# Key-gradient sums' tiles take the merged turns, and query-major scores are issued ahead of some bursts

## The chip, the cores and the metric

The kernel runs on one core of one Trainium2 chip. The metric is the device time of one execution in microseconds (us). Times before: 2569.83 us, the median of 3 runs (2568.68 to 2576.49). One further execution was taken with the hardware profiler; every row shown below comes from it.

## The reference

The reference computes a block and all of its gradients. The block mixes an attention layer and a long convolution of a state-space layer with a gate, for 2048 tokens of 576 channels:

```
g = sigmoid(sum(x * gate_w))                      # one gate per token
a = attention(x, wqkv, wo)                        # 32 heads of 18 channels, softmax over 2048 keys, no mask
b = long_convolution(u, A, B, C, log_dt) + u * Dskip
out = g * a + (1 - g) * b
```

It returns `out` and the gradients with respect to x, wqkv, wo, the six matrices of the state-space layer, log_dt, Dskip and gate_w, given the gradient of `out`. The change touches only the attention's backward pass. There, for each head, the kernel needs, with S the scores, P = exp(S) and dO the output's gradient (already divided by the softmax sums, with the row's correction in an extra channel):

```
dV = P^T dO        dS = P * (V dO^T)        dQ = dS K * scale        dK = dS^T Q
```

## The kernel before, in words

**Tiling.** The heads go in 8 groups of 4 (`NG`), the queries in 4 blocks of 512 (`NQ`, `KB`). A pair (group, query block) is a unit; there are 32 units (`units`), and each takes 32 steps (`NST`). One loop over `G` (from L1359 on) runs all of them, 1024 steps (`NTOT`) and a drain. The forward half of a unit runs at step `G`, its backward half `OFF` = 39 steps later, so that in the middle of the stage each step holds the forward work of one unit and the backward work of an earlier one. A channel group of one head takes 32 rows of the array, so four heads lie side by side (`row`, `tile_position`).

**One step.** The program writes out the order of each engine by hand (`manual_schedule` for TensorE, ScalarE, VectorE, GpSimd and SP), so the order of the code is the order of each engine's queue. A step issues to TensorE:

1. Key-major scores of the forward half, two heads (kind "P1"; `ps_P<-QaT_g,KaT_g` in the profile's names). ScalarE turns them into `PT` = exp(scores), L1475.
2. The first of two products V dO^T (`p2(0)`, "P2"; `ps_P<-dOaT,VaT_g`).
3. A burst or another insertion that depends on the slot, `slot = (G2 + 1) % 8` with `G2 = G - OFF` (below).
4. Query-major scores of the backward half, recomputed from Q and K, two heads (kind "P3"; `ps_P<-KaT_g,QaT_g`). ScalarE turns them into `eb`, L1480, which the sums of dV read.
5. The second product V dO^T (`p2(1)`), then matmuls left over from a burst (`late`).
6. In four of eight steps (G mod 8 in 0, 3, 4, 7, which are slots 2, 5, 6 and 1) the forward output P V, 4 matmuls (`accO`).

VectorE multiplies each product V dO^T with `PT` and writes `ds` (L1485), two a step; between the two it evacuates what the burst left. SP transposes `ds` by DMA (`dsT<-ds`, L1495), three or four blocks of a tile; the blocks left over go through TensorE and VectorE (`turn`, L1112 and L1118).

**Slots.** Eight steps handle one block of 512 keys of a unit. Slots 0 and 1 hold the two halves of the sums for dV (`dv_half`, `accV`), slots 2 and 3 those for dQ (`dq_half`, `accQ`), slots 5 and 6 those for dK (`dk_half`, `accK`); slots 4 and 7 hold `turn`. In step G mod 32 = 5 the `turn` also transposes the output's gradient (`do_tile`), in step G mod 32 = 2 the forward output is turned instead (`accF`).

**PSUM.** It is fully divided: two score tiles of two banks (`S`, taken in turn by P1 and P3, so that P1 needs the tile that `PT` of the step before has read, and P3 the one that `eb` of the step before has read), two banks for V dO^T (`dP`), one for the forward output (`accO`) and one (`accB`) for all bursts and turns. The first half of a burst can write `accB` only when VectorE has evacuated what was there.

**Gradients of K and V.** The sums over the four query blocks of a group are held in SBUF, in `dvacc` and `dkacc` (float32, 4 buffers each, one for each block of 512 keys). With the last query block, the evacuation adds the final part and writes bfloat16 into the two halves of the `dvacc` tile. `store_grad` (L1080) then lets SP turn both with one DMA transpose (L1083, the "merged turn"), and GpSimd packs each half into `dtk` (L1088) and stores it (L1089), 4 and 6 steps after the turn was issued (`packs`). The turn is issued 11, 19, 18 and 18 steps after the sum's last burst for the four key blocks of a group (2 steps in the last group). It is written to `gT`, of which there is one buffer. The dQ of the last two units go the same way.

Of the kernel before, what the change touches and what calls it, by code (L numbers as in the profile page):

```python
# [11 lines left out]
BF = mybir.dt.bfloat16  # L12
F32 = mybir.dt.float32
# [4 lines left out]
P = 128  # L18


def build(tc, aps, dbg_aps=None, stages=("s1", "attn", "post", "s4", "final")):
# [39 lines left out]
    with ExitStack() as gctx:  # L61
# [889 lines left out]
        if "attn" in stages:  # L951
# [7 lines left out]
            with ExitStack() as ctx:  # L959
# [117 lines left out]

                    return t_.bitcast(BF)[:, 0:KB]

                def store_grad(gb, g, whichs, t0):  # L1080
                    n = len(whichs)
                    gT = work.tile([P, 2 * TPQ, 4, HP], BF, tag="gT", bufs=1, name="gT")[:, 0:n * TPQ]
                    nc.sync.dma_start_transpose(out=gT.rearrange("p t a b -> p t (a b)"), in_=gb)  # L1083

                    def pack(x):
                        c0 = whichs[x] * D + g * 4 * DH
                        dtk = work.tile([P, TPQ, 4, DH], BF, tag="dtk", bufs=2, name="dtk")
                        nc.gpsimd.tensor_copy(dtk, gT[:, x * TPQ:(x + 1) * TPQ, :, 0:DH])  # L1088
                        nc.gpsimd.dma_start(dqkv_d[:, t0:t0 + TPQ, c0:c0 + 4 * DH], dtk.rearrange("p t a b -> p t (a b)"))  # L1089
                    for x in range(n):  # L1090
                        packs.append((now[0] + 4 + 2 * x, lambda x=x: pack(x)))
                    packs.sort(key=lambda e: e[0])
# [51 lines left out]
                def gb_tile():  # L1144

                    U, g, b = gq.pop(0)
                    gb = U.pop("dqa")
                    dtk = work.tile([P, TPQ, 4, DH], BF, tag="dtk", bufs=2, name="dtk")
# [17 lines left out]
                def at(n, f):  # L1166
                    todo.setdefault(n, []).append(f)

                def accB(name):
                    return apsp.tile([P, KB], F32, tag="accB", name=name)  # L1170

                fill_r = ident_bf.unsqueeze(1).to_broadcast([P, 4, P])
# [56 lines left out]
                def dk_half(g, b, kq, h, acc):  # L1229
                    U = UN[(g, b)]  # L1230
                    o_ = acc[:, 2 * h * P:2 * (h + 1) * P]
                    for qb in range(TPQ):
                        for j in range(4):
                            mm(o_[HP * j:HP * (j + 1), :].rearrange("p (a b) -> p a b", b=P), lhsT=grp_t[g]["Qtok", b][:, qb, HP * j:HP * (j + 1)],
                               rhs=U["dsT", 2 * kq + h][:, :, j * TPQ + qb, :], start=(qb == 0), stop=(qb == TPQ - 1), tile_position=(0, HP * j))

                    def ev():
                        if b == 0:
                            DKV[("k", g, kq)] = work.tile([P, KB], F32, tag="dkacc", bufs=4, name="dkacc")
                            nc.vector.tensor_copy(DKV[("k", g, kq)], acc)  # L1240
                            return
                        a_ = o_ = DKV[("k", g, kq)]
                        if b == NQ - 1:
                            DKV.pop(("k", g, kq))
                            o_ = DKV[("v", g, kq)].bitcast(BF)[:, KB:2 * KB]
                        nc.vector.tensor_tensor(o_, a_, acc, op=A.add)
                    return ev
# [111 lines left out]
                for G in range(NTOT + OFF + 24):  # L1359
# [34 lines left out]
                    evs, late = [], []  # L1394
                    slot = (G2 + 1) % 8
                    m_ = (G2 - (7, 8, 8, 8, 8, 8, 8, 0)[slot]) // 8
                    if ("f1", G) in todo:
                        acc = apsp.tile([P, KB], F32, tag="accO", name="accF")
                        evs.append(todo.pop(("f1", G))[0](acc))
                        e_done[0] += 1.4  # L1400
                    elif G == NST + 5:
                        evs.append(turn(*do_tile(UN[units[0]])))
                    elif 0 <= m_ < NTOT // 8:
                        u_, kq = divmod(m_, NQ)
                        g, b = units[u_]
                        if slot in SLOTS:
                            nm, burst, h = SLOTS[slot]
                            if h == 0:
                                acc = accB("acc" + nm)
                                fill(acc, NFILL[nm])  # L1410
                                burst(g, b, kq, 0, acc)
                            else:
                                evs.append(burst(g, b, kq, 1, acc))
                                if nm == "Q" and kq == NQ - 1 and u_ < NU - 2:
                                    gq.append((UN[(g, b)], g, b))
                                elif nm == "Q" and kq == NQ - 1:
                                    at(("pre", G + 2), lambda g=g, b=b: store_grad(UN[(g, b)].pop("dqa"), g, (0,), b * TPQ))
                                elif nm == "K" and b == NQ - 1:
                                    at(("pre", G + (2 if g == NG - 1 else (11, 19, 18, 18)[kq])), lambda g=g, kq=kq: store_grad(DKV.pop(("v", g, kq)).bitcast(BF), g, (2, 1), kq * TPQ))
                        else:  # L1420
                            p = 2 * kq + (slot == 4)
                            t_, o_ = ds_tiles((g, b), p) if by_pe((g, b), p) else ([], [])
                            if p == 1 and gq:
                                t2, o2 = gb_tile()
                                t_, o_ = t2 + t_, o2 + o_
                            if G % NST == 5 and G // NST - 1 < NU:
                                t2, o2 = do_tile(UN[units[G // NST - 1]])
                                t_, o_ = t2 + t_, o2 + o_
                            evs.append(turn(t_, o_))
                    if r2:  # L1430
                        g, b, s2 = r2
                        T = grp_t[g]
                        U = UN[(g, b)]
                        par_ = (s2 + OFF) % 2
                        kq, ii = s2 // 8, (s2 % 8) // 2
                        ps = s_pair("P3")
                        if not r1 and s2 % 2:
                            fill(ps[:, 1, :], 1)
                        for x, w in enumerate((KT, KB)):
                            row(ps[:, x, KB - KT if x == 0 else 0:KB], T["QaT", b][:, ii * P:(ii + 1) * P], T["KaT", kq][:, 0:w], par_ + 2 * x)  # L1440
                        rows.append(("P3", g, b, (kq, ii), par_, ps))
                        p2(1)
                    for f in late:
                        f()
# [519 lines left out]
```

## Time and profile before

| What | Value |
|---|---|
| Median of 3 runs | 2569.83 us |
| Profiled execution, its own time | 2574.3 us |
| Its span | 2572.5 us |
| TensorE busy (weight loads apart) | 2246.0 us, 87% |
| VectorE busy | 2277.3 us, 89% |
| ScalarE busy | 2257.6 us, 88% |
| GpSimd busy | 1825.5 us, 71% |
| Granted TensorE clock, mean | 0.976 |

In the profile PE is TensorE, DVE VectorE, ACT ScalarE, POOL GpSimd, SPq the queue of SP that issues DMAs. Row groups give: line, engine, operation, output and inputs by the program's names, shapes, count; then busy us, mean ns of one; then the idle time of the engine just before them and what ended it. A timeline row gives start and duration in us, the engine, the line, the operation, and in brackets the idle time before it and its releaser. All matmuls of the helper `mm` have line 30; they are told apart by their tiles. A duration on ScalarE runs from the start to the last write, and consecutive ones overlap. The first `PT` starts at 124.76 us, the first `eb` at 178.39 us, the last `eb` ends at 1983.6 us; before that stage lie projections, behind it the state-space gradients and the output.

### The profile page before, as it was taken

The page shows a single profiled execution, that of the slowest core. Times are in us where ns is not written, and L with a number is a line of the kernel's source. Part 1 is how long each engine was busy: PE and PEld are TensorE (multiplying, and loading weights), DVE is VectorE, ACT ScalarE, POOL GpSimd, SP SyncE. Part 2 cuts the span into 40 slices and gives each one's busy share as a digit, 9 for nine tenths or more (in the row PEclk, how much of TensorE's full clock was granted, in tenths as well). Part 3 has the DMA queues.
Part 4 walks back from the last instruction along what each step waited for, and adds up shares of the span by engine and source line. Part 5 has one row for each costly group of instructions (what it writes and reads, how often), then busy time and mean ns, then how long its engine had stood idle before and what let it go on. Part 6 is the DMA issues. An engine that isn't in the chain of part 4 may idle for free. (4 is left out here: it accounts for less than half of the span.)

```text
span 2572.5 us, 72343 instructions
## 1 busy us (share of the span) xinstructions
PE 2246.0 (87%) x28463; PEld 1164.1 (45%) x28463; DVE 2277.3 (89%) x4121; ACT 2257.6 (88%) x2760; POOL 1825.5 (71%) x2829
## 2 busy tenths in 40 slices
PE   8988888888888888888888888888888899999989
PEld 4433333333333333333333333333334799998666
DVE  4849999899899989999999999999997799999964
ACT  5579999999999999999999999999987699998221
POOL 0379988888899888989888988898851155555331
PEclk8989999999999999999999999999999799999999
DMA  7749999999999999999999999999979799997995
GB/s 236 190 128 182 184 186 203 200 181 196 202 193 188 196 204 187 191 214 191 185 200 196 182 196 209 185 184 200 195 161 207 189 257 259 257 256 239 277 255 130
DMA packets 1272236, 519.05 MB, mean 202 GB/s; under 512 B 1187041, under 2 KB 1224530, under 8 KB 1269590
## 3 DMA queue, kind: packets, MB, share of 16 engines
q1 hardware_dynamic: 1223974, 368.17, 75.1%
q0 software_dynamic: 45904, 140.73, 20.0%
q10 hardware_dynamic: 2016, 5.51, 0.7%
q8 instruction: 223, 3.65, 0.6%
q14 instruction: 119, 0.97, 0.1%
HBM read 149.42 MB, written 96.94 MB: 96 GB/s over the span
## 5 line engine op out<-in xcount | busy, mean ns | idle before, releaser
L1485 DVE TENSOR_TENSOR ds<-ps_P,PT 128x512 bf16<-128x512 f32 x2048 | 1321.1, 684 | 63.1 <-PE ps_P L30 53.0
L1475 ACT ACTIVATE PT<-ps_P 128x1024 bf16<-128x1024 f32 x1024 | 1110.2, 1085 | 16.8 <-PE ps_P L30 14.9
L1480 ACT ACTIVATE eb<-ps_P 128x896 bf16<-128x896 f32 x1024 | 994.5, 972 | 29.5 <-PE ps_P L30 28.9
L30 PE MATMUL ps_P<-dOaT,VaT_g 32*128 32x512 bf16 x2048 | 786.8, 386 | 3.1 <-DVE ds L1485 2.1
L30 PE MATMUL ps_P<-QaT_g,KaT_g 32*128 32x512 bf16 x2048 | 404.5, 385 | 202.5 <-ACT PT L1475 172.5
L507 POOL TENSOR_TENSOR et<-eG,eT 128x448 f32<-128x448 f32 x576 | 543.3, 964 | 10.7
L30 PE MATMUL ps_P<-KaT_g,QaT_g 32*128 32x384 bf16 (+1 forms) x2048 | 402.5, 361 | 4.4 <-ACT eb L1480 0.8
L30 PEld LDWEIGHTS <-KaT_g 32*128 32x128 bf16 x2048 | 161.4, 91 | 491.6 <-issue 468.4
L507 POOL TENSOR_TENSOR Eo<-et,et 128x448 bf16<-128x448 f32 x288 | 327.4, 1137 | 20.5
L30 PE MATMUL accO<-PT,Vtok_g 128*32 128x512 bf16 x2048 | 213.2, 394 | 3.4 <-DMA Vtok_g<-QKV_d 2.9
L30 PEld LDWEIGHTS <-QaT_g 32*128 32x128 bf16 x2048 | 106.9, 91 | 240.3 <-issue 203.4
L30 PE MATMUL accV<-eb,dOa 128*32 128x384 bf16 (+1 forms) x2048 | 184.0, 366 | 9.3 <-DVE dsT L1118 8.5
L30 PEld LDWEIGHTS <-VaT_g 32*128 32x128 bf16 x2048 | 184.2, 91 | 3.6 <-issue 2.0
L30 PE MATMUL accQ<-ds,Ktok_g 128*32 128x512 bf16 x2048 | 158.4, 386 | 24.5 <-DVE dvacc L1208 18.7
L30 PE MATMUL accK<-dsT,Qtok_g 128*32 128x256 bf16 x4096 | 160.8, 278 | 18.9 <-DMA dsT<-ds 16.6
L30 PEld LDWEIGHTS <-dOa 128*32 128x32 bf16 x3072 | 78.1, 95 | 124.0 <-issue 89.3
L1118 DVE COPY dsT<-turn_p 128x1024 bf16<-128x1024 bf16 (+1 forms) x216 | 130.9, 606 | 1.2 <-PE turn_p L1112 1.2
L1112 PE MATMUL turn_p<-ident_bf,ds 128*128 128x128 bf16 x1552 | 126.6, 222 | 1.7 <-DVE gb L1226 1.0
L673 ACT COPY E1e<-etp 128x1024 bf16<-128x1024 bf16 x132 | 125.2, 1065 | 1.9 <-PE etp L672 1.8
L30 PEld LDWEIGHTS <-Qtok_g 128*32 128x32 bf16 x4096 | 87.6, 96 | 86.5 <-issue 72.9
L507 POOL TENSOR_TENSOR et<-eT 128x32 f32<-128x32 f32 (+3 forms) x288 | 116.1, 423 | 11.4
L560 POOL DMA_DIRECT2D E_d<-Eo x144 | 85.1, 591 | 42.8 <-POOL Eo L507 42.8
(306 smaller groups left out, 3796.8 us busy)
## 6 DMA issues: line engine op xcount, KB each, us to landing
E_d<-Eo POOLq DMA_DIRECT2D x144, 256.0 KB, 3.7
E1n<-E_d POOLq DMA_DIRECT2D x30, 1024.0 KB, 6.5
T0w<-Kp_d SPq DMA_DIRECT2D x18, 1024.0 KB
xs<-xb_d POOLq DMA_DIRECT2D x28, 512.0 KB, 10.3
dsT<-ds SPq DMA_TRANSPOSE x512
dqkv_d<-dtk POOLq DMA_DIRECT2D x96, 72.0 KB, 4.4
Md_d<-mst SPq DMA_DIRECT2D x18, 288.0 KB
skw<-Md_d SPq DMA_DIRECT2D x72, 64.0 KB
```

The lines of the kernel that those rows point to most:

```text
L30: return nc.tensor.matmul(out, lhsT=lhsT, rhs=rhs, start=start, stop=stop, **kw)
L507: nc.gpsimd.tensor_tensor(out, a, b, op=op)
L560: nc.gpsimd.dma_start(E_d[:, q // EQ, 0:EQ * 2 * P], Eo.pop(q).rearrange("p c r n -> p (c r n)"))
L673: copy(E_[:, 4 * q:4 * q + 4], pt_)
L1112: nc.tensor.transpose(pt_[:, x, qb, :], t_[:, qb * P:(qb + 1) * P], ident_bf)
L1118: (nc.scalar.copy if NTOT <= now[0] < NTOT + OFF else nc.vector.tensor_copy)(o_(), src_)
L1475: nc.scalar.activation(U["PT"][i, j // 2], ps, ACT.Exp)
L1480: nc.scalar.activation(e, ps.rearrange("p x q -> p (x q)")[:, KB - KT:2 * KB], ACT.Exp)
L1485: nc.vector.tensor_tensor(U["ds"][i][:, j, :], ps, U["PT"][i, j // 2][:, j % 2, :], op=A.mult)
```

## The change

It has two parts.

**Turns.** `store_grad` takes an optional tile `into`. The four merged turns of a group are written into the `dkacc` tile of the same key block, viewed as bfloat16 (its float32 content has been read by the last addition); `dk_half` keeps that tile under the key `("t", g, kq)` for it. `gT` is left for the two dQ turns and is half as large. `dtk` has 3 buffers in place of 2. The turns are issued 11, 13, 17 and 17 steps after the last burst in place of 11, 19, 18 and 18.

**Scores.** Part 3 of a step becomes a function `bursts`. Where the step has a backward half and its slot is 0, 2 or 5 (first half of a burst), or G mod 32 is 5, the query-major scores are issued first, then the burst, then the second product V dO^T. In all other steps the order is as it was. The order on ScalarE and VectorE is unchanged.

```diff
-                def store_grad(gb, g, whichs, t0):
+                def store_grad(gb, g, whichs, t0, into=None):
                     n = len(whichs)
-                    gT = work.tile([P, 2 * TPQ, 4, HP], BF, tag="gT", bufs=1, name="gT")[:, 0:n * TPQ]
+                    if into is None:
+                        gT = work.tile([P, TPQ, 4, HP], BF, tag="gT", bufs=1, name="gT")
+                    else:
+                        gT = into.bitcast(BF).rearrange("p (t a b) -> p t a b", a=4, b=HP)
                     nc.sync.dma_start_transpose(out=gT.rearrange("p t a b -> p t (a b)"), in_=gb)
...
-                        dtk = work.tile([P, TPQ, 4, DH], BF, tag="dtk", bufs=2, name="dtk")
+                        dtk = work.tile([P, TPQ, 4, DH], BF, tag="dtk", bufs=3, name="dtk")
...
                         if b == NQ - 1:
-                            DKV.pop(("k", g, kq))
+                            DKV[("t", g, kq)] = DKV.pop(("k", g, kq))
                             o_ = DKV[("v", g, kq)].bitcast(BF)[:, KB:2 * KB]
...
-                    if ("f1", G) in todo:
-                        acc = apsp.tile([P, KB], F32, tag="accO", name="accF")
...
+                    def bursts():
+                        nonlocal acc
+                        if ("f1", G) in todo:
+                            acc = apsp.tile([P, KB], F32, tag="accO", name="accF")
...
-                                    at(("pre", G + (2 if g == NG - 1 else (11, 19, 18, 18)[kq])), lambda g=g, kq=kq: store_grad(DKV.pop(("v", g, kq)).bitcast(BF), g, (2, 1), kq * TPQ))
+                                        at(("pre", G + (2 if g == NG - 1 else (11, 13, 17, 17)[kq])), lambda g=g, kq=kq: store_grad(DKV.pop(("v", g, kq)).bitcast(BF), g, (2, 1), kq * TPQ, DKV.pop(("t", g, kq))))
...
+                    behind = r2 and (slot in (0, 2, 5) or G % NST == 5)
+                    if not behind:
+                        bursts()
                     if r2:
                         g, b, s2 = r2
                         T = grp_t[g]
...
                         rows.append(("P3", g, b, (kq, ii), par_, ps))
+                        if behind:
+                            bursts()
                         p2(1)
```

More of the change, by code (lines that the diff above doesn't have):

```diff
@@ L1147, in gb_tile @@
                     gb = U.pop("dqa")
-                    dtk = work.tile([P, TPQ, 4, DH], BF, tag="dtk", bufs=2, name="dtk")
+                    dtk = work.tile([P, TPQ, 4, DH], BF, tag="dtk", bufs=3, name="dtk")
                     packs.append((now[0] + 2, lambda: nc.gpsimd.dma_start(dqkv_d[:, b * TPQ:(b + 1) * TPQ, g * 4 * DH:(g + 1) * 4 * DH],
@@ L1170, in accB @@
                     return apsp.tile([P, KB], F32, tag="accB", name=name)
+                acc = None
                 fill_r = ident_bf.unsqueeze(1).to_broadcast([P, 4, P])
@@ L1396, in build @@
                     m_ = (G2 - (7, 8, 8, 8, 8, 8, 8, 0)[slot]) // 8
-                    if ("f1", G) in todo:
-                        acc = apsp.tile([P, KB], F32, tag="accO", name="accF")
[L1399 to L1411, printed above, removed]
-                            else:
[L1413 to L1418, printed above, removed]
-                                    at(("pre", G + (2 if g == NG - 1 else (11, 19, 18, 18)[kq])), lambda g=g, kq=kq: store_grad(DKV.pop(("v", g, kq)).bitcast(BF), g, (2, 1), kq * TPQ))
[L1420 to L1429, printed above, removed]
@@ new lines, in bursts @@
+                    def bursts():
+                        nonlocal acc
+                        if ("f1", G) in todo:
+                            acc = apsp.tile([P, KB], F32, tag="accO", name="accF")
+                            evs.append(todo.pop(("f1", G))[0](acc))
+                            e_done[0] += 1.4
+                        elif G == NST + 5:
+                            evs.append(turn(*do_tile(UN[units[0]])))
+                        elif 0 <= m_ < NTOT // 8:
+                            u_, kq = divmod(m_, NQ)
+                            g, b = units[u_]
+                            if slot in SLOTS:
+                                nm, burst, h = SLOTS[slot]
+                                if h == 0:
+                                    acc = accB("acc" + nm)
+                                    fill(acc, NFILL[nm])
+                                    burst(g, b, kq, 0, acc)
+                                else:
+                                    evs.append(burst(g, b, kq, 1, acc))
+                                    if nm == "Q" and kq == NQ - 1 and u_ < NU - 2:
+                                        gq.append((UN[(g, b)], g, b))
+                                    elif nm == "Q" and kq == NQ - 1:
+                                        at(("pre", G + 2), lambda g=g, b=b: store_grad(UN[(g, b)].pop("dqa"), g, (0,), b * TPQ))
+                                    elif nm == "K" and b == NQ - 1:
+                                        at(("pre", G + (2 if g == NG - 1 else (11, 13, 17, 17)[kq])), lambda g=g, kq=kq: store_grad(DKV.pop(("v", g, kq)).bitcast(BF), g, (2, 1), kq * TPQ, DKV.pop(("t", g, kq))))
+                            else:
+                                p = 2 * kq + (slot == 4)
+                                t_, o_ = ds_tiles((g, b), p) if by_pe((g, b), p) else ([], [])
+                                if p == 1 and gq:
+                                    t2, o2 = gb_tile()
+                                    t_, o_ = t2 + t_, o2 + o_
+                                if G % NST == 5 and G // NST - 1 < NU:
+                                    t2, o2 = do_tile(UN[units[G // NST - 1]])
+                                    t_, o_ = t2 + t_, o2 + o_
+                                evs.append(turn(t_, o_))
```

## The prediction

> **What bounds the kernel now.** First the page: the span and the costliest groups (busy us, mean ns | idle before, releaser).
>
> ```profile
> span 2572.5 us, 72343 instructions
> ...
> L1475 ACT ACTIVATE PT<-ps_P 128x1024 bf16<-128x1024 f32 x1024 | 1110.2, 1085 | 16.8 <-PE ps_P L30 14.9
> L1480 ACT ACTIVATE eb<-ps_P 128x896 bf16<-128x896 f32 x1024 | 994.5, 972 | 29.5 <-PE ps_P L30 28.9
> ...
> L30 PE MATMUL ps_P<-QaT_g,KaT_g 32*128 32x512 bf16 x2048 | 404.5, 385 | 202.5 <-ACT PT L1475 172.5
> ...
> L30 PE MATMUL ps_P<-KaT_g,QaT_g 32*128 32x384 bf16 (+1 forms) x2048 | 402.5, 361 | 4.4 <-ACT eb L1480 0.8
> ```
>
> Two exponentials a step, 1024 steps, fill ScalarE, and the key-major scores (`ps_P<-QaT_g,KaT_g`, "P1") wait 172.5 us for it: in the attention stage TensorE follows ScalarE. I then read ScalarE in the timeline, eight steps apart (first two columns: start and duration, us):
>
> ```profile
> 1000.71 1.08 ACT L1480 ACTIVATE eb<-ps_P 128x896 bf16<-128x896 f32 x1
> 1001.51 1.20 ACT L1475 ACTIVATE PT<-ps_P 128x1024 bf16<-128x1024 f32 x1
> 1002.59 0.92 ACT L1480 ACTIVATE eb<-ps_P 128x896 bf16<-128x896 f32 x1
> 1003.41 1.03 ACT L1475 ACTIVATE PT<-ps_P 128x1024 bf16<-128x1024 f32 x1
> ...
> 1015.32 1.20 ACT L1475 ACTIVATE PT<-ps_P 128x1024 bf16<-128x1024 f32 x1
> ```
>
> The records overlap, so I read their ends: 1001.79, 1002.71, 1003.51, 1004.44, ..., 1016.52. Eight steps take 13.81 us, 1.726 a step, in a fixed rhythm: `eb` ends 0.81 after `PT`, the next `PT` 0.92 after that. The late start of `eb` at 1002.59 costs nothing; it still ends 0.80 after `PT`. So the 28.9 us that `eb` waits for scores are mostly no loss. What is lost shows against this rhythm in the middle of the stage (300 to 1900 us):
>
> ```profile
> L1475 ACT ACTIVATE PT<-ps_P 128x1024 bf16<-128x1024 f32 x911 | 991.2, 1088 | 2.6 <-PE ps_P L30 1.8
> ```
>
> ```profile
> 1100.00:1500.00 400.00, 342.40 (x4316) 135.70 (x4308) 376.16 (x636) 396.40 (x457) 349.74 (x569) 0.99 1.04 194
> ```
>
> 1600 us by 911 steps is 1.756, 0.030 over the rhythm. Over the 985 steps that have both kinds of scores that is 30 us: the most that removing stalls can win there. The second row is a window of 400 us: VectorE busy 376, ScalarE 396, TensorE clock 0.99.
>
> **The reordered scores.** One step that will change, slot 5 (first half of the key sums, with the PV matmuls):
>
> ```profile
> 1005.11 1.05 ACT L1475 ACTIVATE PT<-ps_P 128x1024 bf16<-128x1024 f32 x1
> 1006.01 0.96 ACT L1480 ACTIVATE eb<-ps_P 128x896 bf16<-128x896 f32 x1
> 1006.81 1.08 ACT L1475 ACTIVATE PT<-ps_P 128x1024 bf16<-128x1024 f32 x1
> ```
>
> ```profile
> 1006.21 0.39 PE L30 MATMUL ps_P<-QaT_g,KaT_g 32*128 32x512 bf16 x2 [0.46 <-ACT PT L1475]
> 1006.22 0.39 PE L30 MATMUL ps_P<-dOaT,VaT_g 32*128 32x512 bf16 x1
> 1006.53 0.62 PE L30 MATMUL accK<-dsT,Qtok_g 128*32 128x256 bf16 x16
> 1007.09 0.39 PE L30 MATMUL ps_P<-KaT_g,QaT_g 32*128 32x384 bf16 x2
> 1007.11 0.37 PE L30 MATMUL ps_P<-dOaT,VaT_g 32*128 32x512 bf16 x1
> 1007.41 0.40 PE L30 MATMUL accO<-PT,Vtok_g 128*32 128x512 bf16 x4
> 1007.94 0.39 PE L30 MATMUL ps_P<-QaT_g,KaT_g 32*128 32x512 bf16 x2
> ```
>
> P1 starts at 1006.21, 0.05 after the previous `PT` ended (1005.11 + 1.05 = 1006.16): it needs that score tile. The query-major scores ("P3") need the other one, which `eb` leaves at 1006.97, so they can't start before 1007.02, 0.81 after P1. They start at 1007.09 now, because the burst of 0.56 us fills the wait exactly. Moved ahead, P3 gains 0.07 us here, and TensorE, which takes matmuls in order (slot 2 below shows it), stands idle for 0.49 us (0.81 less the 0.32 from P1 to its follower) with burst, second P2 and PV queued behind. The second P2 also loses its partner: now it starts 0.02 after P3 on other rows of the array and takes no time; behind the burst it runs alone. Each unit shows what a P2 alone costs:
>
> ```profile
> 1021.07 0.39 PE L30 MATMUL ps_P<-KaT_g,QaT_g 32*128 32x384 bf16 x2
> 1021.48 0.37 PE L30 MATMUL ps_P<-dOaT,VaT_g 32*128 32x512 bf16 x1
> 1021.78 0.40 PE L30 MATMUL accO<-PT,Vtok_g 128*32 128x512 bf16 x4
> 1022.11 0.39 PE L30 MATMUL ps_P<-QaT_g,KaT_g 32*128 32x512 bf16 x2
> ```
>
> ```profile
> 1020.62 1.08 ACT L1475 ACTIVATE PT<-ps_P 128x1024 bf16<-128x1024 f32 x1
> ...
> 1022.54 1.02 ACT L1475 ACTIVATE PT<-ps_P 128x1024 bf16<-128x1024 f32 x1
> ```
>
> P2 to PV 0.30, PV to P1 0.33. And here TensorE overran: P1 came 0.41 after `PT` ended (1021.70), and the next `PT` ended at 1023.56, 1.45 after P1 began, 1.86 after the last one, 0.13 late. At 1006.21 P1 was 1.68 ahead of its `PT`'s end (1007.89), so P1 may slip by 0.23 us; all beyond it delays ScalarE.
>
> Slots 2 and 5 after the change, P1 to P1: 0.81 to P3, 0.32 to the burst (the step from P1 to its follower), 0.55 burst, 0.30 P2, 0.33 PV: 2.31 us. That is 0.58 over 1.73, less 0.23: 0.35 us late, twice in eight steps. Slot 0 has no PV: 1.98, 0.25 over, 0.02 to 0.03 late. Together 0.73 us in eight steps; the other steps have no spare ScalarE time to give it back. 985 steps are 123 periods: **+90 us**. The unknown is the P2 behind a burst: 0 if it hides beside a neighbour (0.05 late, twice: +12), 0.40 as after the late P3 above (0.45 late twice, 0.13 in slot 0: +127). I take 0.30, the row nearest to it, PV behind.
>
> What the move was to save, in slot 2:
>
> ```profile
> 1000.88 0.69 DVE L1208 TENSOR_TENSOR dvacc<-dvacc,accV 128x512 f32<-128x512 f32 x1 [0.36 <-PE accV L30]
> ...
> 1001.62 0.61 PE L30 MATMUL accQ<-ds,Ktok_g 128*32 128x512 bf16 x8 [0.20 <-DVE dvacc L1208]
> 1002.17 0.39 PE L30 MATMUL ps_P<-KaT_g,QaT_g 32*128 32x384 bf16 x2
> ```
>
> The burst waits for the bank until 1001.57; P3, whose own tile was free by 1001.84 (1001.79 + 0.05), stands behind it and is late by 0.33, yet `eb` ends in time (above). Saved: nothing that ScalarE shows.
>
> The step with G mod 32 = 5 puts P3 ahead of 12 transposes (8 take the 0.55 of a burst, so 0.83): 0.81 + 0.32 + 0.83 + 0.30 = 2.26, 0.30 late by the same rule, 31 times: +9, less 4 of today's 30 us, an estimate for its wait on the output's gradient: **+5** (0 to +9). After the last P1, 39 steps run without PT; 15 are reordered there, at up to 0.30 for the lone P2: **+2** (0 to +4.5). On VectorE the lone P2 puts off the second `ds` of a changed step by 0.78 us (P2 1.68 after P1, now 0.90). VectorE is busy 13.2 us of the 14.05 that eight steps take on average (376 of 400), and often a `ds` or more behind; in 14.5 us that covers most of it, so I take 0. That cover gone is the third rival.
>
> **The stores.** All four stores of a group go through one `gT`. The waits (us, times, longest), then SP and TensorE in the timeline:
>
> ```profile
> SPq L1083 <- POOL dtk L1088: 24.7, 7, 5.2
> ```
>
> ```profile
> POOL dtk L1088 <- DMA dqkv_d<-dtk: 20.0, 7, 3.8
> ...
> PE accK L30 <- DMA dsT<-ds: 11.9, 8, 3.3
> ```
>
> ```profile
> 1337.35 1.23 SPq L1083 DMA_TRANSPOSE gT<-dvacc  x1
> ```
>
> ```profile
> 1344.24 1.05 PE L30 MATMUL accK<-dsT,Qtok_g 128*32 128x256 bf16 x16 [1.40 <-DMA dsT<-ds]
> ...
> 1345.76 0.62 PE L30 MATMUL accO<-PT,Vtok_g 128*32 128x512 bf16 x4
> 1346.31 0.61 PE L30 MATMUL ps_P<-QaT_g,KaT_g 32*128 32x512 bf16 x2
> ```
>
> SP's queue stood up to 5.2 us on `gT`, and the `dsT` transposes behind it came late; at 1344, behind the turn of 1337, that stopped TensorE. With a tile of its own for each store this wait goes; the number of transposes, packs and stores stays. What remains are `dsT` transposes that merely land behind a store; three of the four stores go out 1 to 6 steps earlier. A third `dtk` lifts POOL's 20.0 us; POOL sets nothing in the steps read above, so 0. The key sums' tiles now stay held until POOL's second pack, 15 to 23 steps after the sum; the next group writes them 32 steps after, 9 steps (16 us) to spare; were that gone, `dkacc` would stand on VectorE with `ds` behind it. Gain: at least 0, at most the 30 us; I take a little over the 11.9 us of late key bursts, **-12 us**.
>
> Sum against the profiled execution (2574.3 us, span 2572.5): 90 + 5 + 2 - 12 = +85, 2659. The median of the runs shown is 4.5 lower, 2569.83: **2655 us**.
>
> **Rivals.**
> 1. The P2 is free behind a burst. Then slots 2 and 5 lose 0.05 each: +12 and -12, about 2570. For it: it runs beside P3 now. Against it: the 0.30 of 1021.48 to 1021.78.
> 2. Faster. The late `dsT` is what costs the stage its 30 us, and the reordered steps have room: it decides if what follows P3 in slots 2 and 5 fits in 1.15 us (1.73 + 0.23 - 0.81) where I count 1.50. Then the waits go and nothing is paid: 2570 - 25 = 2545. For it: 24.7 us on SP, and TensorE's 172.5 us of waiting. Against: that waiting lies ahead of P1, and P3 ahead of the burst doesn't reach it.
> 3. VectorE joins. If it stands the whole 0.78 us three times in eight steps and makes nothing up: 13.2 busy, 0.84 idle as now and 2.34 are 16.4 us, 2.6 over 13.81, times 123: +320, less 12: 2878; anything above 2700 counts here. For it: 94% busy. Against: work that it has put off fills such waits.
> 4. The clock falls. After the stop at 1344 the PV to P1 step takes 0.55 (1345.76 to 1346.31) instead of 0.33. If the added gaps of 0.49 us did that all the time, TensorE's phases per period (8 of P1 at 0.32, 8 of P3 at 0.31, 8 bursts at some 0.55, 4 PV at 0.33, 3 P2 at 0.30: 11.7 us) would become 19.5 and bound it: +700, 3270. Against: gaps of 0.46 stand ahead of P1 in some 375 of 1024 steps already (172.5 by 0.46), at a clock of 0.99. The Trainium skill, "TensorE: Matmul & The Clock Gate", has both: by "Part 1: The HAM clock gate" it takes an idle window of about 3.4 us to throttle, so nothing would change; by "A second HAM failure mode: psum-queue depth-cycling" frequent micro-idles between matmul groups are enough. The trace sides with the first.
> 5. The engines' order doesn't follow the code, and only the stores change: 2558. Against: the order above is that of the loop, matmul by matmul.
>
> **Chances.** Forecast (2615 to 2700) 0.63; between it and 2585 0.04; rival 1 0.10 (half of it within 0.3%); rival 2 0.11; rival 3 0.07; rival 4 0.02; rival 5 0.03 (faster). 0.3%, 8 us, is about what a measurement of this kernel tells from no change. Faster: 0.11 + 0.03 + 0.02 = 0.16; same 0.06; slower 0.78. 8 in 10 lies between 2557 (forecast, the gap below it, rivals 1 and 5: 0.80) and 2705; the likeliest's own range is 2615 to 2700, from the bounds of P2 and of the stores.
>
> **What will show it.** P3's group should wait for `eb` some 150 to 180 us (0.49 in three steps of eight), near 0 now; P1's wait for `PT` shrink; ScalarE idle ahead of `PT`, 16.8 us now, grow to 60 or more, put down to PE; eight steps take 14.5 us by `PT`'s ends; SP's wait for `dtk` be gone. Wrong I am if those eight steps still take 13.8, or if P2 starts within 0.1 of the burst's end without moving PV.

## The result, and the profile after

The changed kernel takes 2926.8 us (median of 6 runs, 2904 to 2951) against 2569.9 (6 runs, 2569 to 2584): a ratio of 1.136 [1.133, 1.140] (the brackets are a 95% interval). Ratios, here and below, leave out executions more than 1.5% above the fastest of their kernel, so a ratio can be smaller than the quotient of the two medians. Slower was forecast, but 85 us slower; it is 357. The time is above the whole range. In the profiled executions (2940.9 and 2574.3 us) all of the difference lies in the attention stage: from the `PT` of step 39 to that of step 1023 it takes 2097.8 us, where it took 1731.0.

The page of the changed kernel, with the rows that answer to those of before (`PT` is line 1487 now, `eb` 1492; busy us, mean ns | idle before, releaser):

```profile
span 2939.2 us, 72323 instructions
...
PEclk9976877878696868787787869686878989999999
...
L1497 DVE TENSOR_TENSOR ds<-ps_P,PT 128x512 bf16<-128x512 f32 x2048 | 1346.0, 684 | 358.4 <-PE ps_P L30 308.0
L1487 ACT ACTIVATE PT<-ps_P 128x1024 bf16<-128x1024 f32 x1024 | 1054.4, 1030 | 255.9 <-PE ps_P L30 253.8
L1492 ACT ACTIVATE eb<-ps_P 128x896 bf16<-128x896 f32 x1024 | 950.4, 929 | 101.4 <-PE ps_P L30 100.7
...
L30 PE MATMUL ps_P<-KaT_g,QaT_g 32*128 32x512 bf16 (+1 forms) x2048 | 473.6, 416 | 129.2 <-ACT eb L1492 128.1
L30 PE MATMUL ps_P<-QaT_g,KaT_g 32*128 32x512 bf16 x2048 | 513.5, 453 | 70.6 <-ACT PT L1487 68.9
```

The waits moved as foretold: the query-major scores ("P3"), 0.8 us before, wait 128 us for `eb`; the key-major scores ("P1") wait 69 us for `PT` instead of 172; ScalarE idles 256 us ahead of `PT` instead of 17, put down to TensorE. But two things do not belong to the forecast. The scores' matmuls themselves became longer (P1 385 to 453 ns, P3 361 to 416). And the row of the clock (40 slices of the span) shows 6 to 8 tenths through most of the attention stage, where before it showed 8 or 9:

```profile
PEclk8989999999999999999999999999999799999999
```

The window of 400 us that stood at 0.99 before reads, in the changed kernel:

```profile
1100.00:1500.00 400.00, 361.58 (x3546) 123.25 (x3544) 318.31 (x522) 337.45 (x376) 290.44 (x477) 0.79 0.81 157
```

So there are two losses, and the trace has stretches of each.

**At full clock the forecast period is there.** TensorE in slot 5 (P1, P3, burst, second P2, PV, next P1), and ScalarE eight steps apart:

```profile
1110.59 0.39 PE L30 MATMUL ps_P<-QaT_g,KaT_g 32*128 32x512 bf16 x2 [0.41 <-ACT PT L1487]
...
1111.40 0.39 PE L30 MATMUL ps_P<-KaT_g,QaT_g 32*128 32x384 bf16 x2 [0.42 <-ACT eb L1492]
1111.72 0.62 PE L30 MATMUL accK<-dsT,Qtok_g 128*32 128x256 bf16 x16
1112.28 0.39 PE L30 MATMUL ps_P<-dOaT,VaT_g 32*128 32x512 bf16 x1
1112.59 0.40 PE L30 MATMUL accO<-PT,Vtok_g 128*32 128x512 bf16 x4
1112.92 0.39 PE L30 MATMUL ps_P<-QaT_g,KaT_g 32*128 32x512 bf16 x2
```

```profile
1107.79 1.02 ACT L1487 ACTIVATE PT<-ps_P 128x1024 bf16<-128x1024 f32 x1 [0.25 <-PE ps_P L30]
...
1122.36 1.02 ACT L1487 ACTIVATE PT<-ps_P 128x1024 bf16<-128x1024 f32 x1 [0.26 <-PE ps_P L30]
```

P1 to P3 0.81, to the burst 0.32, to P2 0.56, to PV 0.31, to P1 0.33: 2.33 us where 2.31 was counted. The period is 14.57 us (1108.81 to 1123.38, ends of `PT`); 14.5 was forecast.

**At half clock TensorE's matmuls take 1.5 to 1.8 times as long.** Here the clock's record changes from 1.00 to 0.50 at 1056.64:

```profile
1055.86 0.39 PE L30 MATMUL ps_P<-QaT_g,KaT_g 32*128 32x512 bf16 x2
...
1056.67 0.61 PE L30 MATMUL ps_P<-KaT_g,QaT_g 32*128 32x384 bf16 x2 [0.17 <-ACT eb L1492]
1057.21 1.04 PE L30 MATMUL accK<-dsT,Qtok_g 128*32 128x256 bf16 x16
1058.19 0.60 PE L30 MATMUL ps_P<-dOaT,VaT_g 32*128 32x512 bf16 x1
1058.72 0.62 PE L30 MATMUL accO<-PT,Vtok_g 128*32 128x512 bf16 x4
1059.27 0.61 PE L30 MATMUL ps_P<-QaT_g,KaT_g 32*128 32x512 bf16 x2
```

```profile
1059.91 1.02 ACT L1487 ACTIVATE PT<-ps_P 128x1024 bf16<-128x1024 f32 x1 [1.57 <-PE ps_P L30]
```

P1 to P1 takes 3.41 us (1055.86 to 1059.27), and ScalarE waits 1.57 us. TensorE now sets the pace, not ScalarE: the median of eight steps that lie wholly at half clock is 21.09 us. Added up from the clock's records in the trace, the stage has 909.6 us at half clock in 57 spells; before it had 49.3 us in 5.

The account, an estimate for the two profiled executions, which lie 367 us apart: the period costs (14.58 - 13.81) x 123 = +95 us; half clock, taken at the period above, loses (21.09 - 14.58) / 21.09 = 0.31 of its time, 281 us, less some 15 us of the same in the kernel before; the stores give 12 back (below). That makes 349 of the 367 us; the other 18 are not accounted for. Nearly three quarters of the loss is the clock, which the forecast gave a chance of 0.02.

### The profile page after: what moved, and what is told of

Read it like the earlier page. It is cut to its first block, busy times and chain, and to the rows that moved or that the text cites. A ratio compares the mean times of both kernels' runs of the same rounds, so it can differ in the third digit from the quotient of the medians.

```text
span 2939.2 us, 72323 instructions
## 1 busy us (share of the span) xinstructions
PE 2668.7 (91%) x28463; PEld 1223.0 (42%) x28463; DVE 2321.9 (79%) x4121; ACT 2312.9 (79%) x2760; POOL 1821.3 (62%) x2829
## 4 chain that ended last, share of the span: by engine, by line
PE 53%; ACT 24%; DVE 15%; issue 5%; DMA 2%; SPq 1%; POOL 0%; ACTq 0%; DVEq 0%; POOLq 0%
PE ps_P L30 21%; ACT eb L1492 14%; ACT PT L1487 8%; PE accK L30 6%; PE accO L30 6%; PE accQ L30 4%; PE turn_p L1115 3%; DVE ds L1497 3%; DVE tz L734 3%; DVE wab L754 3%; PE accV L30 3%; PE ps_dx L30 2%; DVE tz L737 2%; DVE HG L739 2%; DVE Rw L759 1%
## 5 line engine op out<-in xcount | busy, mean ns | idle before, releaser
L1487 ACT ACTIVATE PT<-ps_P 128x1024 bf16<-128x1024 f32 x1024 | 1054.4, 1030 | 255.9 <-PE ps_P L30 253.8
L1492 ACT ACTIVATE eb<-ps_P 128x896 bf16<-128x896 f32 x1024 | 950.4, 929 | 101.4 <-PE ps_P L30 100.7
L30 PE MATMUL ps_P<-dOaT,VaT_g 32*128 32x512 bf16 x2048 | 841.0, 454 | 2.0 <-DVE ds L1497 1.5
L30 PE MATMUL ps_P<-KaT_g,QaT_g 32*128 32x512 bf16 (+1 forms) x2048 | 473.6, 416 | 129.2 <-ACT eb L1492 128.1
L30 PE MATMUL ps_P<-QaT_g,KaT_g 32*128 32x512 bf16 x2048 | 513.5, 453 | 70.6 <-ACT PT L1487 68.9
L507 POOL TENSOR_TENSOR et<-eG,eT 128x448 f32<-128x448 f32 x576 | 542.0, 961 | 10.2
L30 PEld LDWEIGHTS <-QaT_g 32*128 32x128 bf16 x2048 | 138.3, 95 | 423.4 <-issue 395.8
L30 PE MATMUL accO<-PT,Vtok_g 128*32 128x512 bf16 x2048 | 260.3, 483 | 1.9 <-DMA Vtok_g<-QKV_d 1.4
L30 PE MATMUL accK<-dsT,Qtok_g 128*32 128x256 bf16 x4096 | 220.5, 354 | 5.1 <-DMA dsT<-ds 3.9
L1115 PE MATMUL turn_p<-ident_bf,ds 128*128 128x128 bf16 x1552 | 159.3, 259 | 4.7 <-DVE gb L1230 4.3
L1115 PEld LDWEIGHTS <-ds 128*128 128x128 bf16 x1552 | 119.3, 116 | 61.7 <-issue 61.7
L1121 DVE COPY dsT<-turn_p 128x1024 bf16<-128x1024 bf16 (+1 forms) x216 | 131.4, 608 | 11.8 <-PE turn_p L1115 11.4
```

Of the source, the lines that this page charges most:

```text
L30: return nc.tensor.matmul(out, lhsT=lhsT, rhs=rhs, start=start, stop=stop, **kw)
L507: nc.gpsimd.tensor_tensor(out, a, b, op=op)
L1487: nc.scalar.activation(U["PT"][i, j // 2], ps, ACT.Exp)
L1492: nc.scalar.activation(e, ps.rearrange("p x q -> p (x q)")[:, KB - KT:2 * KB], ACT.Exp)
```

## The experiments

In the expectations, "the stage" and "eight steps" mean what they mean above. The time beside each run is the median of its executions, and the ratio is to the kernel before on the same chip. "Eight steps" is the median where they lie wholly at full clock. The totals of half clock are added up from the clock's records as above.

### The two parts apart

The stores alone: the kernel before with `store_grad`, the third `dtk`, `DKV["t"]` and the new delays, its scores as they were.

```
-def store_grad(gb, g, whichs, t0):
+def store_grad(gb, g, whichs, t0, into=None):
...
-    gT = work.tile([P, 2 * TPQ, 4, HP], BF, tag="gT", bufs=1, name="gT")[:, 0:n * TPQ]
+    if into is None:
+        gT = work.tile([P, TPQ, 4, HP], BF, tag="gT", bufs=1, name="gT")
+    else:
+        gT = into.bitcast(BF).rearrange("p (t a b) -> p t a b", a=4, b=HP)
...
-    DKV.pop(("k", g, kq))
+    DKV[("t", g, kq)] = DKV.pop(("k", g, kq))
```

> The kernel before with the first part of the change alone: merged turns into the key sums' tiles, turns at 11, 13, 17, 17 steps, three dtk buffers; scores in their old order. Theory (the stores remove SP's wait and some late transposes): 2558 us, 12 below the kernel before, granted clock 0.976 or a little more, since fewer key bursts stand for the DMA. Rival (the irregular losses re-form elsewhere): 2570. A second rival, that the stores cause part of the 357 us: above 2600.

Measured: 2560.0 us, ratio 0.996 [0.995, 0.998]; eight steps 13.81, stage 1722.7. As expected, and the fastest of all that ran. On SP the stores' transposes no longer wait for POOL's `dtk` (24.7 us before), and in the middle of the stage (300 to 1900 us) the key bursts' wait for late transposes, 11.9 us in 8 places before, is

```profile
PE accK L30 <- DMA dsT<-ds: 5.3, 3, 3.3
```

So that row, which the forecast named, is 6.6 us shorter, and the stage 8.3. How much of the 8.3 is due to it is not shown: the profiled stage also has 11.8 us less at half clock (37.5 in place of 49.3). The wait did not vanish: three transposes still came late.

The scores alone: the changed kernel with these lines taken back, two `dtk` and the delays of before, so that this is left of the change:

```
+behind = r2 and (slot in (0, 2, 5) or G % NST == 5)
+if not behind:
+    bursts()
...
+    if behind:
+        bursts()
     p2(1)
```

> The changed kernel with its first part taken back: old gT, old turn steps, two dtk buffers; scores ahead of the bursts in slots 0, 2, 5 and in step G mod 32 = 5. Theory (the order of the scores is the whole loss): 2920 to 2950 us at a granted clock near 0.83, as the changed kernel. Rival (both parts are needed for the loss): under 2800.

Measured: 2914.1 us, 1.133 [1.131, 1.136], just under the 2920 to 2950 expected; 867 us at half clock, eight steps 14.58. Both parts of the loss, the longer period and the half clock, belong to the order of the scores.

### Is the clock a cause, or only a sign?

Matmuls that do nothing useful (identity times a matrix, 128x128x512, into the bank that the next transposes overwrite) ahead of each `turn` make TensorE's work longer and its gaps shorter. If the low clock only went along with the loss, this can but cost.

```
 def turn(tiles, outs):
+    if OFF <= now[0] < NTOT:
+        fill(accB("warm"), 2)
```

> The changed kernel with two idle-filling matmuls (128x128 by 512 columns, into the accumulator bank, overwritten by what follows) ahead of the transposes of each turn in slots 4 and 7, where TensorE stands some 0.4 us a step anyway; nothing reads them. Clock theory: in the changed kernel the granted clock falls to half in 3.41 us windows in which TensorE streams too little, and that makes some 270 of the 357 us; the overrun of slots 2 and 5 makes the other 90. Then the added work lifts the quiet windows, the clock comes back to 0.95 or more and the kernel falls to 2650 to 2700 us. Rival (the clock follows the waits and isn't their cause; the added order alone loses the time): 2920 us or more, since TensorE has more to do.

```profile
span 2742.7 us, 73183 instructions
...
L30 PE MATMUL ps_P<-KaT_g,QaT_g 32*128 32x384 bf16 (+1 forms) x2048 | 406.1, 358 | 191.0 <-ACT eb L1494 188.8
```

```profile
1100.00:1500.00 400.00, 350.40 (x4004) 130.50 (x4005) 347.49 (x576) 367.87 (x415) 323.13 (x526) 0.99 0.93 180
```

Measured: 2754.2 us, 1.068 [1.063, 1.074]. With more to do it is 173 us faster than the changed kernel; the clock is back at 0.99, with 37.5 us of half clock in the whole stage. The clock is a cause. The expected 2650 to 2700 was missed by what the fills cost: two of them take 0.65 us and delay the steps behind the turns, so that eight steps take 15.45 us, 0.87 more than 14.58, 107 us in 123 periods. 173 and 107 make 280 us that the clock had cost by this run, close to the 281 of the account. P3's wait, 188.8 us in this kernel of full clock, is also the figure to hold against the 150 to 180 of the forecast.

With one fill in place of two:

> The changed kernel with one idle-filling matmul in place of two ahead of the transposes of each turn in slots 4 and 7 (nothing reads it). With two, the clock came back (0.981), but the fills made TensorE overrun in those slots as well: eight steps took 15.45 us in place of 14.58. One fill takes some 0.33 of the 0.4 us that TensorE idles there. Clock theory: granted clock 0.95 or more, eight steps at 14.6 us, 2630 to 2670 us, which is what the prediction's own sum gives. Rival (one fill leaves windows that are too quiet): clock near 0.9, 2750 to 2850.

Measured: 2892.9 us, 1.114 [1.108, 1.120], 586 us at half clock. That is above both the expected 2630 to 2670 and the rival's 2750 to 2850. One fill was not enough, and cost 0.43 us in eight steps.

The same single fill in the kernel with the stores alone, to see if that one still loses anything to the clock:

> The kernel before with the stores' part of the change, and one idle-filling matmul ahead of each turn in slots 4 and 7. Theory (the few half-clock stretches that follow late transposes last shorter or don't come): 2545 to 2558 us. Rival (the fills cost as much as they save, or those stretches come from stops of over 2 us, which a fill doesn't shorten): 2555 to 2570, as the stores alone.

Measured: 2607.8 us, 1.013 [1.011, 1.015]. Half clock in the stage falls from 37.5 to 13.9 us, but eight steps take 14.20 us; 0.39 x 123 = 48 is paid to save a few us, so both the expected 2545 to 2558 and the rival's 2555 to 2570 were too low.

### The lone second product

The second P2 ahead of the burst, beside the scores again:

```
+  p2(1)
   if behind:
       bursts()
-  p2(1)
```

> The changed kernel with the second V dO^T product issued right behind the scores, ahead of the burst, so that it runs beside them again. By the sum of the prediction slots 2 and 5 then overrun by 0.05 us in place of 0.35 and slot 0 not at all: +12 us for the scores and -12 for the stores, about 2570, if the clock holds. Theory that the gap ahead of the scores halves the clock by itself: the gap stays (0.42 us in three of eight steps), granted clock 0.85 or less, 2800 us or more. Theory that it takes the overrun's longer period and the gap together: clock 0.95 or more, 2560 to 2600.

Measured: 2707.8 us, 1.054 [1.049, 1.059]; eight steps 14.32 us, 310 us at half clock. Neither expectation came out: the time lies between the 2560 to 2600 of the one and the 2800 or more of the other, and so does the profiled execution's clock, 0.926. The period is shorter than 14.58, but not the 13.9 that two overruns of 0.05 us would make: at full clock `PT`'s step in slot 6 went from 2.11 to 1.86 us, that in slot 3 stayed at 2.09. TensorE and VectorE in slot 2:

```profile
800.43 0.39 PE L30 MATMUL ps_P<-KaT_g,QaT_g 32*128 32x384 bf16 x2 [0.41 <-ACT eb L1492]
800.87 0.37 PE L30 MATMUL ps_P<-dOaT,VaT_g 32*128 32x512 bf16 x1
801.17 0.61 PE L30 MATMUL accQ<-ds,Ktok_g 128*32 128x512 bf16 x8
```

```profile
799.52 0.69 DVE L1212 TENSOR_TENSOR dvacc<-dvacc,accV 128x512 f32<-128x512 f32 x1 [0.26 <-PE accV L30]
800.13 1.88 DVE L1497 TENSOR_TENSOR ds<-ps_P,PT 128x512 bf16<-128x512 f32 x3
```

P2 starts 0.44 behind P3, not 0.02, because its own bank was not free: the first of the three `ds` behind the evacuation ends at 800.82 in the trace, 0.05 before P2 starts, and the trace puts 15.4 us of TensorE's idle time ahead of matmuls into `ps_P` down to `ds`, 39 times. Before, the burst covered that time too.

### Which of the moved gaps brings the clock down

Slot 0 alone is reordered (`behind = r2 and slot == 0`), with the stores. By the account of the path it costs almost nothing, because slot 0 has no PV.

> The changed kernel with the scores moved ahead in slot 0 alone (no PV there). The gap of 0.42 us ahead of the scores is made in one step of eight, but TensorE ends in time for the next step (overrun 0.02 to 0.03 by the prediction). Theory that overrun and clock need slots 2 and 5: eight steps at 13.8 us, granted clock 0.97 or more, 2555 to 2570. Rival (a gap behind an idle stretch is enough for the clock: slot 7 and slot 0 have no PV and are the quietest pair): clock under 0.9, 2700 or more.

Measured: 2731.7 us, 1.062 [1.059, 1.064], with 511 us at half clock in 53 spells and a clock of 0.891. The expected 2555 to 2570 was wrong; the rival's forecast (clock under 0.9, 2700 or more) came true. Eight steps at full clock take 14.09, 0.28 more than before, which is 34 of the 172 us above the stores alone; the other 138 are put down to the clock. TensorE in slot 0, behind the turn of slot 7:

```profile
1846.46 0.39 PE L30 MATMUL ps_P<-QaT_g,KaT_g 32*128 32x512 bf16 x2 [0.46 <-ACT PT L1487]
...
1847.27 0.39 PE L30 MATMUL ps_P<-KaT_g,QaT_g 32*128 32x384 bf16 x2 [0.41 <-ACT eb L1492]
...
1850.79 0.62 PE L30 MATMUL accQ<-ds,Ktok_g 128*32 128x512 bf16 x8 [0.24 <-DVE dvacc L1212]
```

P1 already waited 0.46 us here. The moved gap of 0.41 stands 0.8 us behind it. (The last row is where the 0.28 us come from: the sums of slots 0 and 1 now end later, VectorE leaves the bank later, and slot 2's burst with P3 behind it is late; `PT`'s step is 1.73 us in slots 0 and 1 and 1.99 in slot 3. The sum for slot 0 had left that out.) Slot 2 and slot 5, one at a time, tell whether it is the new gap or the pair that matters (the diff for slot 2; the other kernel has `slot == 5`):

```
-  behind = r2 and (slot in (0, 2, 5) or G % NST == 5)
+  behind = r2 and slot == 2
```

> The stores as changed; the scores ahead of the burst in slot 2 alone (the step where the burst itself waited 0.20 us for VectorE to leave the bank, so where the move was to save something). Theory A (activity within a few microseconds decides the clock): slot 2 lies between busy pairs (slot 1 with PV, slot 3 with PV), its one gap of 0.49 us stays spread out, and the clock stays above 0.96 in the stage; then eight steps take 13.81 + 0.36 (the overrun that slot 3 shows in the changed kernel) = 14.17 us and the time is 2560 + 123 x 0.36 = about 2604. Theory B (any new gap behind P1 lets the clock fall): like the kernel with slot 0 alone, hundreds of microseconds at half clock, 2680 to 2780.

> The stores as changed; the scores ahead of the burst in slot 5 alone. The overrun is 0.38 us in eight steps (slot 6 of the changed kernel), 14.19 us by PT's ends, 2560 + 123 x 0.38 = about 2607 at full clock. Theory A (activity within a few microseconds decides): slot 5 is followed by slot 6 with its burst, the first two steps behind the turn of slot 4; the gap of slot 5 comes 1.7 us after the gap in slot 4, so some loss of clock, less than with slot 0 alone: 2607 to 2680. Theory B (any new gap lets the clock fall): as with slot 0 alone, 2680 to 2780.

Measured: slot 2 alone 2614.5 us, 1.017 [1.014, 1.020], 61 us at half clock; slot 5 alone 2805.8 us, 1.082 [1.078, 1.086], 558 us at half clock in 75 spells (the profiled execution, 2777, was the fastest of four). At full clock both have the same period, 14.20 and 14.19, as counted for one late step. Slot 2 came out 11 us above the 2604 of the theory that activity within a few microseconds decides; slot 5 lies well beyond the 2607 to 2680 that the same theory gave, so its size was underrated there, and the rival's 2680 to 2780 was nearer. The rival itself, that any new gap does it, is out by slot 2. TensorE with slot 2 alone (every idle time that the rows show between 1102.5 and 1109):

```profile
1103.37 0.39 PE L30 MATMUL ps_P<-QaT_g,KaT_g 32*128 32x512 bf16 x2
...
1104.18 0.39 PE L30 MATMUL ps_P<-KaT_g,QaT_g 32*128 32x384 bf16 x2 [0.42 <-ACT eb L1492]
...
1107.20 0.39 PE L30 MATMUL ps_P<-QaT_g,KaT_g 32*128 32x512 bf16 x2 [0.24 <-ACT PT L1487]
...
1108.93 0.39 PE L30 MATMUL ps_P<-QaT_g,KaT_g 32*128 32x512 bf16 x2 [0.40 <-ACT PT L1487]
```

With slot 5 alone:

```profile
1101.90 0.39 PE L30 MATMUL ps_P<-QaT_g,KaT_g 32*128 32x512 bf16 x2 [0.37 <-ACT PT L1487]
...
1103.63 0.39 PE L30 MATMUL ps_P<-QaT_g,KaT_g 32*128 32x512 bf16 x2 [0.46 <-ACT PT L1487]
...
1104.44 0.60 PE L30 MATMUL ps_P<-KaT_g,QaT_g 32*128 32x384 bf16 x2 [0.42 <-ACT eb L1492]
```

In slot 2 the moved gap has PV on both sides (that of slot 1 before it, that of slot 2 itself behind it; slot 3 has none, other than the expectation says), and P1 ahead of it waited for nothing. In slot 5 it is the third within 3 us: 0.37 ahead of the turn's P1, 0.46 ahead of slot 5's P1, 0.42 ahead of P3; and the P3 behind it already takes 0.60, at half clock. In stretches of 3.41 us, which is the step on which all changes of clock in the records fall, the same kernel reads (second number: TensorE busy, then the others; clock third from the end):

```profile
1097.65:1101.07 3.42, 3.22 (x40) 0.90 (x37) 3.04 (x6) 3.42 (x5) 3.32 (x5) 1.00 1.09 252
1101.07:1104.48 3.41, 2.17 (x26) 0.92 (x22) 3.41 (x7) 3.41 (x5) 3.25 (x4) 1.00 1.21 130
1104.48:1107.89 3.41, 3.41 (x34) 1.10 (x37) 1.40 (x3) 1.85 (x3) 2.80 (x11) 0.50 0.91 234
1107.89:1111.31 3.42, 3.42 (x37) 1.40 (x30) 2.63 (x5) 2.75 (x3) 1.45 (x5) 0.50 0.03 8
1111.31:1114.72 3.41, 2.62 (x39) 1.20 (x37) 3.13 (x5) 3.04 (x4) 0.00 (x0) 1.00 0.65 146
```

One stretch with 2.17 us of work, and the next two are at half clock.

### A longer period with the old order

Is it just that ScalarE got slower and TensorE idles more? In the kernel before, ScalarE does 400 columns of `PT` twice in slots 3 and 6, which lengthens the period without moving a matmul:

```
+ if 0 <= G2 and G < NTOT and slot in (3, 6):
+     nc.scalar.activation(U["PT"][i, j // 2][:, 0, 0:400], ps[:, 0, 0:400], ACT.Exp)
```

> The kernel before, order of the scores as it was; in slots 3 and 6 ScalarE computes the first 400 columns of PT a second time (same values), which delays it by some 0.35 us in just the two steps in which the changed kernel delays it. It asks whether the longer period alone makes TensorE quiet enough. Theory that period and moved gaps act together: eight steps at 14.5 us, granted clock 0.96 or more, about 2640 us. Rival (any stretch to 14.5 us lets the clock fall): clock under 0.9, 2750 or more.

Measured: 2698.2 us, 1.049 [1.045, 1.052]; eight steps 14.88, 165 us at half clock in 28 spells. The period was stretched by more than the 14.5 intended, so the time lies above the expected 2640, but it stays under the rival's 2750 and the clock, 0.958, near the 0.96. The period explains it all: 1.07 x 123 = 132 us against 125 measured. A longer period than the changed kernel's, with idle time ahead of P1 of 0.91 us in slot 4 and 0.67 in slot 7 (medians), has a fifth of the time at half clock (165 us against 910), and that costs next to nothing, since ScalarE is what everything waits for. Here 0.91 us ahead of slot 4's P1 and 0.45 ahead of slot 5's follow each other too, more than the 0.37, 0.46 and 0.42 above, so idle time added up is not the whole rule (see the last section).

### The steps with G mod 32 = 5 alone

With the stores, only `behind = r2 and G % NST == 5`.

> The stores as changed; the scores ahead of the burst only in the 31 steps with G mod 32 = 5, where the burst is 12 transposes. By the prediction: 0 to 9 us slower than the stores alone (2560), so 2560 to 2569, as the lone P2 puts these steps 0.30 us late. Rival: the wait of these transposes for the output's gradient no longer holds P3 up, which saves up to 4 us: 2556 to 2560.

Measured: 2567.3 us, 0.998 [0.996, 1.000], eight steps 13.81. That is 7 us above the stores alone (on another chip), in line with the +5 (0 to +9) of the sum, but the two intervals overlap, and the profiled execution has 25 us more at half clock, so its size is not settled. The trace shows the step itself: behind the reordered one (G mod 32 = 7) `PT`'s step at full clock is 2.03 us, 0.30 late as counted, which makes 8.4 us in the 28 such steps; in the kernel with the stores alone, steps G mod 32 = 6 and 7 together were 5.0 us late. Nothing that ran beats the stores alone.

## Why the prediction was right and wrong

**Right: the path at full clock.** Slots 2 and 5 late by 0.35 each: by `PT`'s steps 2.09 and 2.11 instead of 1.73, 0.36 and 0.38 late, and 1.73 in slot 0's. A lone P2 for 0.30: 0.31. The eight steps: 14.58 for 14.54 (13.81 and 0.73). The reordered scores: +95 for +90. P3's wait of 150 to 180 us: 189 where the clock held, 128 where for nearly half of the stage TensorE was behind and P3 found `eb` done. The stores: -12 for -12, of which the wait that was named can have made about half. The wait for `dvacc`, which the move was to save: gone with slot 2 alone (0.2 us left of 18.7), and nothing gained by it, as argued. Rivals 1, 2, 3 and 5 fall with the same rows: P2 is not free, nothing is faster, VectorE idles 308 us for TensorE in the changed kernel rather than holding it up, and the order follows the code.

**Wrong: rival 4 was dismissed.** The step that failed is its "against": gaps of 0.46 stand ahead of P1 in some 375 steps already, at a clock of 0.99. That took the presence of gaps as proof that more of the same do no harm, and so the sum has no term for the clock, which cost some 270 us by the account above. It did not ask where the new gaps lie. The row that rival 4 starts from, at 1345.76, stands itself in a spell at half clock of the trace before (1343.95 to 1354.19 in the clock's records), which the mean of 0.99 hides. In that trace the idle time ahead of P1 (300 to 1900 us, gaps over 0.1) has a median of 0.37 us in slot 4, 0.46 in slots 5, 0 and 1, 0.13 in slots 6 and 7, and none in slots 2 and 3. The change sets new gaps in slots 5 and 0, right behind old ones, and one in slot 2, where there was none. How little an average tells can be read in one long spell at full clock of the changed kernel, with its last stretches:

```profile
1101.01:1155.62 54.61, 47.19 (x554) 17.27 (x555) 50.05 (x84) 52.42 (x61) 38.57 (x65) 1.00 0.85 164
```

```profile
1107.84:1111.25 3.41, 2.50 (x28) 0.94 (x21) 3.37 (x6) 3.41 (x5) 3.10 (x5) 1.00 0.97 252
...
1148.80:1152.21 3.41, 3.23 (x38) 0.85 (x33) 3.18 (x5) 3.16 (x4) 3.01 (x5) 1.00 0.89 195
1152.21:1155.62 3.41, 2.34 (x30) 1.09 (x30) 3.41 (x8) 3.41 (x5) 3.24 (x5) 1.00 1.22 223
1155.62:1159.04 3.42, 3.42 (x43) 1.11 (x35) 1.60 (x4) 2.19 (x3) 3.05 (x4) 0.50 0.85 70
```

TensorE is busy 47.19 of 54.61 us, 86%; before it was 342.40 of 400, also 86%. The mean did not change. What changed is how uneven it is over a few microseconds: 2.50 us of 3.41 leaves the clock alone, 2.34 is followed by half clock, and that keeps it for 27 us.

Rival 4's own price, 3270, took the whole stage at half clock. It is 909.6 of 2097.8 us, 43%; its period of 19.5 us was 21.09. A chance of 0.02 for a mechanism whose price (+700) was eight times the forecast's (+85) called for a closer look at the trace: the gaps of eight steps, added up over the few microseconds around each moved one, before and after, would have shown the piled-up 1.25 us in slot 5.

The Trainium skill, "TensorE: Matmul & The Clock Gate", was weighed the wrong way. Its section "A second HAM failure mode: psum-queue depth-cycling" says that a TensorE that idles for very short times between groups of matmuls often enough swings between half and full clock. The runs here agree: the changed kernel has 57 spells at half clock in the stage, and in the stretch quoted from the kernel with slot 5 alone no idle time is above 0.46 us. Its section "Part 1: The HAM clock gate" ties the fall to an idle window of about 3.4 us. The length is the step of 3.41 us seen here, but the stretch ahead of a fall was 64 to 69% busy, not idle, by the rows above (2.17 and 2.34 of 3.41).

## What to carry to other kernels

Idle time on TensorE, even where it isn't the bottleneck, was free here only while it was spread out: before moving work on it, add up its work over any 3 to 4 us around the place, before and after, and be wary of a new gap behind an old one. Compare the granted clock of the stage before pricing anything else, and where it fell, test it with a few useless matmuls: if the clock comes back and more work makes the kernel faster, the clock is a cause. Filling is a test, not a cure, where the fills lie on the path (0.65 us for two); here the cure is the old order.

## What the runs showed of the hardware

**The clock has two values and a step of 3.41 us.** In all kernels here the records show 1.00 or 0.50, and each spell but the one that the end cuts off is a whole number of 3.41 us, so that all changes of a run lie on one grid. In the changed kernel the same sequence of spells (54.6 us full, 27.3 half, 10.2 full, 17.1 half, 3.4, 6.8, 10.2, 6.8, and so on) returns every 136.5 us, 40 such steps, over long parts of the stage: the grid runs on by itself and the kernel's period slides along it. That also fits the wider spread of times, 1.6% over six runs instead of 0.6%.

**What lets it fall is close to an amount of work in one such step, but the recorded busy share measures it badly.** Of the full-clock steps of the changed kernel in the stage, all 41 with under 0.70 of recorded busy time were followed by half clock, none of 106 between 0.70 and 0.85, and 15 of 49 between 0.85 and 0.90 (the 15 hold float32 transposes, which the other 34 do not). But the stretched kernel kept its clock in all 50 steps between 0.65 and 0.70 (and lost it in 26 of 42 between 0.60 and 0.65), and the one with two fills in all 13; the one with slot 0 alone lost it in 52 of 84 between 0.70 and 0.75. Counting how much of the array works sorts the steps better. Take the columns that a matmul streams times its share of the 128 x 128 array, both as its row gives them (`32*128 32x512` counts 128), and add them up over each full-clock step of the stage, in all 13 kernels: all 47 steps with under 2400 were followed by half clock, 273 of 778 between 2400 and 3200, and none of 5091 above. Slot 2 alone has no step under 2800, slot 5 alone 54, the changed kernel 43, the kernel before 6. A few matmul records are missing from the traces, and what decides in the middle band was not settled.
